# Packing eight units of a preparation into the rows of six, masks by ScalarE, and loads begun on ScalarE's queue

## The chip, the cores and the metric

The program runs on one core of one Trainium2 chip. Its engines work side by side, each through its own instructions in order: PE (TensorE, matmuls), DVE (VectorE, elementwise work and scans), ACT (ScalarE, copies out of PSUM, activations), POOL (GpSimd) and SP (SyncE, which issues DMAs). ACT can issue DMAs too; a DMA that ACT issues stands among its activations in the same order. The metric is the device time of one execution in microseconds (us), the median of several runs.

## The reference

A gated linear attention with a rank-one state correction (4 batches x 8 heads, 768 tokens, 40 channels) feeds a two-layer network with a spatial gate.

```python
for t in range(S):
    kt, vt, rt = (k[:, :, t], v[:, :, t], r[:, :, t])
    wt, at, bt = (w[:, :, t], a[:, :, t], b[:, :, t])
    y[:, :, t] = np.einsum('bhd,bhde->bhe', rt, state)
    Sa = np.einsum('bhde,bhe->bhd', state, at)
    state_decay = state * wt[:, :, None, :] - np.einsum('bhd,bhe->bhde', Sa, bt)
    state = state_decay + np.einsum('bhd,bhe->bhde', vt, kt)
...
h = np.maximum(x @ w_in, 0.0)
u, v = (h[..., :d_ff // 2], h[..., d_ff // 2:])
v_n = (v - mu) / np.sqrt(var + 1e-06)
v_s = np.einsum('ts,bsd->btd', w_spatial, v_n) + b_spatial[None, :, None]
return ((u * v_s) @ w_out).astype(np.float32)
```

Here x is y with its heads laid side by side, and mu and var are the mean and variance of v over its last axis.

## The kernel before

**Steps.** Phase 1 cuts the 768 tokens into chunks of 64 (C) and treats two batches at a time: 2 x 12 chunks are 24 steps (s, also q). A step has 16 heads, as 8 units (n) of two heads (par): one head lies in partitions 0 to 63, the other in 64 to 127. A head has 40 channels (E), so 40 of each 64 partitions carry data in everything that is laid out by channel; the loads of a preparation bring 48 rows per half, the last 8 being filling.

**Preparation of step q.** `prep_piece` loads the decays w and three other inputs (`oth`) of the step in six pieces of 16 rows. `scan1` and `scan2` form running products of w with two scans over 8 x 66 columns (`S`, `Et`; L292 and L301) and a reciprocal (L296); `at_mul` (L318) and `sl_mul` (L324) multiply `oth` by them into `at` and `sl`. All five run on DVE. `lprime` (L339) multiplies `sl` and `at` on PE into small triangles, and `lblock` (L349) copies them out of PSUM on DVE while it masks them with `maskl` and changes their sign. Four steps form a group; `invert` turns the group's 32x32 triangles into inverses on DVE, 30 rounds of two operations (L363, L367) between transposes. The input tiles `ein` are two, so the load of step q + 2 waits for `sl_mul` of step q. Results of eight steps are kept (`fifo`, and nine `Et`), so preparation runs up to eight steps ahead.

**The step itself.** Matmuls with the state, eviction by ACT, masking by POOL (`strict`, L406), and so on: `c_bp` (L545), `c_ff` (L563), `c_xx` (L581), `c_mp` and `c_y` (L641), with `c_y_out` (L654) writing y on DVE; the next step's `c_bp` follows. Blocks of the next step are made in between: `b_copy` (L392) copies `at` into `At` by DMA, `lin_load` (L381) and `vtok_load` (L384) bring the late inputs from HBM, `b_lka`, `b_h`, `b_tok` and others are matmuls with evictions by ACT.

**The network.** Its first layer (`m_v` L759, `m_u` L712) fills PE from step 11 on, four slots in a step and on beyond step 23; `vr` holds a normalised half before it is stored, in two buffers. `decode` turns the weights, which come as 64-bit numbers, into two floats each on DVE. Phase 2 does the spatial matmuls and the projection.

**Order.** It is written by hand: `at(t, fn, ...)` puts a function at a plan time, in units of a step; the plan is sorted and each engine gets its instructions in that order. `b_copy(q)` stands at q - 0.89, `lin_load(q)` at q - 1.80 and q - 1.66, `vtok_load(q)` at q - 0.52 and q - 0.38, all DMAs of a step on SP's queue. Preparations are placed by `PREP`: 4 and 5 in step 0, 6 and 7 in step 1, 8 and 9 in step 2, 10 and 11 in step 3, from 12 on one in a step. The network's loads and stores, `scn_load`, `scr_store` and `y_store` go through SP too.

Of the kernel before, what the change touches and what calls it, by code (L numbers as in the profile page):

```python
# [18 lines left out]
P = 128  # L19
# [9 lines left out]
EW = WF + 3 * NU * C  # L29
NR = C + E  # L30
# [187 lines left out]
def phase1(ctx, tc, early, late, vtok, win, xs, vns, uts, dscr):  # L218
# [12 lines left out]
    fifo = [pool(f"fifo{i}") for i in range(GS)]  # L231
# [4 lines left out]
    etp = pool("etp", 9)  # L236
# [15 lines left out]
    ein = [p.tile([P, EW], F32, name=f"ein{i}") for i, p in enumerate((pin, pin, extra, extra))]  # L252
# [16 lines left out]

    def prep_load(s, rows, cols=slice(0, EW), i=None, queues=(nc.sync, nc.sync)):  # L270
        t = ein[s % 2 if i is None else i]
        for par in range(2):
            o = par * 64
            queues[par].dma_start(out=t[o:o + rows, cols], in_=early[par, s, 0:rows, cols])

    def prep_piece(s, k):
        par, r = k % 2, k // 2 * 16
        o = par * 64 + r
        nc.sync.dma_start(out=ein[s % 2][o:o + 16], in_=early[par, s, r:r + 16])

    def scan1(s, i=None):
        t = ein[s % 2 if i is None else i]
        Et = etp.tile([P, WF], F32, name="Et")
        at = fifo[s % 8].tile([P, NU, C], F32, name="at")
        sl = fifo[s % 8].tile([P, NU, 2, C], F32, name="sl")
        wseg = t[:, 0:WF]
        oth = t[:, WF:].rearrange("p (q n c) -> p n q c", q=3, c=C)
        sx = pin.tile([P, WF], F32, name="S", bufs=2)
        sv = sx.rearrange("p (n c) -> p n c", c=WSEG)
        st["pre", s] = (Et, at, sl)  # L290
        st["raw", s] = (wseg, oth, sv)
        nc.vector.tensor_tensor_scan(  # L292
            out=sx[:, ::-1], data0=wseg[:, ::-1], data1=ends[:, ::-1],
            initial=0.0, op0=ALU.mult, op1=ALU.add,
        )
        nc.vector.reciprocal(out=eseg[:, :, 0:1], in_=sv[:, :, 1:2])  # L296

    def scan2(s):
        Et, at, sl = st["pre", s]
        wseg, oth, sv = st["raw", s]  # L300
        nc.vector.tensor_tensor_scan(  # L301
            out=Et, data0=wseg, data1=ends, initial=0.0, op0=ALU.mult, op1=ALU.add,
        )

    def scr_store(s):
        if s % CPB == 0:
            return
        sv = st["raw", s][2]
        sc = jit.tile([P, NU], F32, name="sc")
        nc.scalar.activation(sc, sv[:, :, 1], AF.Copy)  # L310
        for par in range(2):
            nc.sync.dma_start(out=scr[s, par], in_=sc[RR[par]])

    def at_mul(s, eng, ns=slice(0, NU)):
        Et, at, sl = st["pre", s]
        oth = st["raw", s][1]
        Ev = Et.rearrange("p (n c) -> p n c", c=WSEG)
        eng.tensor_tensor(out=at[:, ns], in0=oth[:, ns, 0], in1=Ev[:, ns, 0:C], op=ALU.mult)  # L318

    def sl_mul(s, eng, ns=slice(0, NU)):  # L320
        Et, at, sl = st["pre", s]
        wseg, oth, sv = st["raw", s]
        k = ns.stop - ns.start
        eng.tensor_tensor(  # L324
            out=sl[:, ns], in0=oth[:, ns, 1:],
            in1=sv[:, ns, 2:C + 2].unsqueeze(2).broadcast_to([P, k, 2, C]), op=ALU.mult,
        )

    def lprime(s, units=range(NU)):
# [4 lines left out]
        for n in units:  # L334
            for blk in range(2):
                for par in range(2):
# [3 lines left out]
                        pl[o:o + HB, n, :], lhsT=sl[PR[par], n, par, cs], rhs=at[PR[par], n, cs],  # L340
# [3 lines left out]
    def lblock(s):  # L344
        if s % GS == 0:
            st["Lc", s // GS] = inv.tile([P, GS * NU, HB], F32, name="Lc")
        Lc = st["Lc", s // GS]
        u0 = (s % GS) * NU
        nc.vector.tensor_tensor(  # L349
            out=Lc[:, u0:u0 + NU, :], in0=st.pop(("pl", s)),  # L350
            in1=maskl.unsqueeze(1).broadcast_to([P, NU, HB]), op=ALU.mult,
        )
# [27 lines left out]
    def lin_load(s, par):  # L380
        nc.sync.dma_start(out=lin[s % 2][RR[par], :, 0:LATE], in_=late[par, s])  # L381

    def vtok_load(s, par):
        nc.sync.dma_start(out=Rts[s % 2][par][PR[1 - par], :, C:], in_=vtok[s, par])  # L384

    def b_copy(s, par):
        if par == 0:
            At = [jat.tile([P, NU, C], F32, name=f"At{i}") for i in range(2)]
            tk = jit.tile([P, NU, 2, E], F32, name="tk")
            st["blk", s] = (At, Rts[s % 2], tk, xfs[s % 2])  # L390
        at = st["pre", s][1]
        nc.sync.dma_start(out=st["blk", s][0][par][PR[par]], in_=at[PR[par]])  # L392

    def b_lka(s):
        Et, at, sl = st["pre", s]
        pk = ps_k.tile([P, NU, C], F32, name="bk")
        for n in range(NU):
            for par in range(2):
                nc.tensor.matmul(  # L399
                    pk[PR[1 - par], n, :], lhsT=sl[PR[par], n, 1 - par, :], rhs=at[PR[par], n, :],  # L400
# [10 lines left out]
    def b_lka_out(s, par):  # L411
# [3 lines left out]
        if s in LKA_POOL:  # L415
            nc.scalar.activation(At[par][ev], pk[ev], AF.Copy)  # L416
            strict(At[par][ev], NU)
            return
        nc.vector.tensor_tensor(
            out=At[par][ev], in0=pk[ev],  # L420
            in1=maskp[ev].unsqueeze(1).broadcast_to([64, NU, C]), op=ALU.mult,
        )
# [12 lines left out]
    def b_h_out(s, par):  # L435
        ev = PR[1 - par]
        Rt = Rts[s % 2]
        if s in H_POOL:
            nc.scalar.activation(Rt[par][ev, :, 0:C], st["ph", s][ev], AF.Copy)
            strict(Rt[par][ev, :, 0:C], NU)  # L440
            return
        nc.vector.tensor_tensor(
            out=Rt[par][ev, :, 0:C], in0=st["ph", s][ev],
            in1=maskp[ev].unsqueeze(1).broadcast_to([64, NU, C]), op=ALU.mult,
        )
# [16 lines left out]
    def b_l21(s):  # L462
        Et, at, sl = st["pre", s]
        m1 = ps_k.tile([P, NU, HB], F32, name="bk")
        for n in range(NU):
            for par in range(2):
                o = (1 - par) * 64 + HB
                nc.tensor.matmul(
                    m1[o:o + HB, n, :], lhsT=at[PR[par], n, HB:], rhs=sl[PR[par], n, par, 0:HB],
# [116 lines left out]
    def c_xx_out(s, g):  # L586
# [3 lines left out]
        if s in TRI_POOL:  # L590
            for par in range(2):
                done = nc.scalar.activation(Rt[par][PR[par], gp], xx[PR[1 - par]], AF.Copy, scale=-1.0)  # L592
            marks["a", s] = done.ins
            for par in range(2):
                strict(Rt[par][PR[par], gp, 0:C], NP)
            return
        for par in range(2):
            nc.scalar.activation(Rt[par][PR[par], gp, C:], xx[PR[1 - par], :, C:], AF.Copy, scale=-1.0)
        for par in range(2):
            ur, ev = PR[par], PR[1 - par]  # L600
            nc.vector.tensor_tensor(
                out=Rt[par][ur, gp, 0:C], in0=xx[ev, :, 0:C],
                in1=maskn[ev].unsqueeze(1).broadcast_to([64, NP, C]), op=ALU.mult,
            )
# [41 lines left out]
    def c_y_out(s, g):  # L646
        gp, ns = grp(g)
        c = s % CPB
        Ev = st["pre", s][0].rearrange("p (n c) -> p n c", c=WSEG)
# [54 lines left out]
    def m_v(g, bq, i, k=0):  # L704
# [8 lines left out]
        vr = st["act"].tile([P, DH], F32, name="vr", bufs=2)  # L713
# [65 lines left out]
    H_POOL, LKA_POOL, TRI_POOL = range(0, 99), range(0, 99), range(0, 99)  # L779
# [47 lines left out]
    SCR, SLM = {4: 0.68}, {5: 0.83}  # L827
    PREP = {4: 0.03, 5: 0.45, 6: 1.03, 7: 1.45, 8: 2.03, 9: 2.45, 10: 3.03, 11: 3.45}
    for q in range(GS, NS):
        t = PREP.get(q, q - 8 + 0.01)  # L830
        at(t + 0.20, scan1, q)
        at(t + 0.28, scan2, q)
        at(SCR.get(q, t + 0.285), scr_store, q)
        at(t + 0.29, at_mul, q, AT_ENG)
        at(SLM.get(q, t + 0.30), sl_mul, q, SL_ENG)
        if q + 2 < NS:
            gap = 0.03 if q < 8 else 0.07 if q < 12 else 0.14
            for k in range(6):
# [10 lines left out]
    T_DEC, T_MOE = 4.2, 11  # L849
    for i in range(6):  # L850
        gen = decode(1 - i // 3, i % 3)
        for k in range(8):
            at(T_DEC + i + k * 0.10 - (0.9 if k == 0 else 0), step, gen)
    at(T_DEC + 5.9, open_act)
# [30 lines left out]
    with tc.manual_schedule():  # L885
# [4 lines left out]
        pads(v, ein[1])  # L890
# [7 lines left out]
        pads(p, ein[2])  # L898
        pads(p, ein[3])
        for q, cols in ((0, W), (1, W), (0, O), (1, O), (2, W), (2, O), (3, W), (3, O)):  # L900
            prep_load(q, 48 if q else 64, cols, q, qs)
# [4 lines left out]
        for m, val in ((maskp, 1.0), (maskn, -1.0)):  # L906
            p.memset(m, val)
            for rows in PR:
                p.affine_select(
                    out=m[rows], in_=m[rows], pattern=[[1, C]], base=0,  # L910
                    channel_multiplier=-1, compare_op=ALU.is_gt, fill=0.0,
                )
        for t in (Mc, *xfs):
# [23 lines left out]
        prep_load(4, 48)  # L937
# [14 lines left out]
        prep_load(5, 48)  # L952
# [73 lines left out]
```

## Time and profile before

| | us |
|---|---|
| median of 3 runs (663.11 to 670.05) | 667.58 |
| the profiled execution | 665.08 |
| its span, first to last instruction | 663.3 |
| busy in it: PE | 571.8 |
| DVE | 448.4 |
| ACT | 384.2 |
| POOL | 225.9 |

The clock granted to PE was 0.943 of full speed on average. An engine's busy time counts its instructions; the issuing of a DMA is counted as the queue's (SPq, ACTq), not as busy time. In rows of groups, the numbers after the bar are the group's busy time, the mean of one instruction in ns, and the idle time of the engine just before them with what ended it. In rows by time, the first number is the start from the span's begin, the second the duration. A row of a stage gives its window, its length, and for each engine the busy time and the instructions, then PE's clock, the DMA engines' busy share and GB/s. The busy shares are averages; what a stage is worth is read inside the stage.

### The profile page before, as it was taken

To read this page: it belongs to the slowest core of one execution; us is meant where nothing else is said; L and a number is where in the kernel's file an instruction comes from. 1 tells how busy PE (TensorE), PEld (TensorE's weight loads), DVE (VectorE), ACT (ScalarE), POOL (GpSimd) and SP (SyncE) were. 2 spreads that over 40 slices of the span, in tenths; PEclk is the share of its full clock that TensorE was granted. 3 is DMA by queue.
4 is the path that set the end of the run, shared out by engine and by line. 5 is a ranking of instruction groups with operands and counts; after the bars stand their busy time and mean duration, and the time that the engine had idled before them with its cause. 6 is when DMAs were issued, how large, how long until landed. Compare 5 with 4: busy or idle time off the path is not lost.

```text
span 663.3 us, 25848 instructions
## 1 busy us (share of the span) xinstructions
PE 571.8 (86%) x10960; PEld 518.3 (78%) x10960; DVE 448.4 (68%) x970; ACT 384.2 (58%) x860; POOL 225.9 (34%) x298
## 2 busy tenths in 40 slices
PE   1447885498777887999999999999989999999997
PEld 1437674487766776888888888888878999999997
DVE  8999789989999999488896677343384842332220
ACT  2135662377666775688878887888765543221212
POOL 6013330224332334144341332332354843352221
PEclk9967997789787898999999999999998999999999
DMA  8654778477555546657565365375395557150001
GB/s 199 121 107 67 134 152 147 70 175 155 135 127 115 131 117 120 142 127 172 154 190 148 86 173 144 90 198 132 89 262 182 162 155 240 61 157 31 31 31 59
DMA packets 106331, 87.68 MB, mean 132 GB/s; under 512 B 35496, under 2 KB 92072, under 8 KB 104296
## 3 DMA queue, kind: packets, MB, share of 16 engines
q1 hardware_dynamic: 105672, 84.31, 52.0%
q10 hardware_dynamic: 544, 1.72, 1.2%
q8 instruction: 86, 1.41, 1.0%
q14 instruction: 29, 0.24, 0.1%
HBM read 59.20 MB, written 20.50 MB: 120 GB/s over the span
## 4 chain that ended last, share of the span: by engine, by line
PE 63%; DVE 15%; DMA 7%; issue 6%; ACT 4%; SPq 3%; POOL 1%; DVEq 0%; ACTq 0%; POOLq 0%
PE po L199 6%; PE pv L759 6%; PE pv L712 6%; PE pg L179 5%; PE pg L180 5%; PE pg L181 5%; PE ch L563 4%; PE bp L545 4%; PE ch L581 4%; PE bk L429 2%; DMA ein<-in_early 2%; DVE itmp L363 2%; PE bk L451 2%; PE bk L399 2%; PE bp L641 2%
## 5 line engine op out<-in xcount | busy, mean ns | idle before, releaser
L406 POOL TENSOR_SCALAR_AFFINE_SELECT Rt<-Rt 64x512 f32<-64x512 f32 (+1 forms) x144 | 83.8, 584 | 156.2 <-ACT Rt L592 128.5
L406 POOL TENSOR_SCALAR_AFFINE_SELECT At<-At 64x512 f32<-64x512 f32 x48 | 41.5, 864 | 164.0 <-ACT At L416 151.9
L555 ACT ACTIVATE Rt<-bp 64x416 f32<-64x416 f32 x96 | 49.1, 511 | 56.2 <-PE bp L545 53.6
L363 DVE TENSOR_TENSOR itmp<-A 128x30 f32<-128x30 f32 (+9 forms) x180 | 66.5, 369 | 3.4
L179 PE MATMUL pg<-wsh,vh 128*128 128x384 f32 x192 | 65.4, 341 | 2.0 <-ACT vh L51 2.0
L545 PE MATMUL bp<-lin,Mc 40*64 40x104 f32 x768 | 47.3, 278 | 22.1 <-DVE y L654 19.8
L183 DVE TENSOR_TENSOR g<-pg,bb 128x384 f32<-128x384 f32 x32 | 17.8, 556 | 70.7 <-PE pg L181 68.4
L180 PE MATMUL pg<-wsl,vh 128*128 128x384 f32 x192 | 65.1, 339 | 0.0
L181 PE MATMUL pg<-wsh,vl 128*128 128x384 f32 x192 | 63.6, 339 | 0.0
L367 DVE TENSOR_TENSOR A<-A,itmp 128x30 f32<-128x30 f32 (+9 forms) x180 | 59.1, 328 | 6.2
L545 PEld LDWEIGHTS bp<-lin,Mc 40*64 40x64 f32 x768 | 40.7, 150 | 25.5 <-DVE y L654 22.7
L563 PE MATMUL ch<-Rt,At 128*64 128x104 f32 x768 | 48.0, 283 | 5.9 <-issue 4.8
L55 POOL TENSOR_TENSOR gl<-g,gh 128x384 fp32r<-128x384 f32 x32 | 33.0, 1035 | 58.1 <-ACT gh L51 58.1
L592 ACT ACTIVATE Rt<-ch 64x416 f32<-64x416 f32 x96 | 49.1, 511 | 4.6 <-PE ch L581 2.2
L563 PEld LDWEIGHTS ch<-Rt,At 128*64 128x64 f32 x768 | 42.2, 157 | 10.4 <-issue 7.1
L51 ACT ACTIVATE gh<-g 128x384 fp32r<-128x384 f32 x32 | 16.7, 521 | 54.3 <-DVE g L184 54.3
L339 PE MATMUL bk<-at,sl 64*32 64x32 f32 x1536 | 21.2, 203 | 26.5 <-DVE sl L324 20.7
L55 POOL TENSOR_TENSOR vl<-raw,vh 128x512 fp32r<-128x512 f32 x24 | 31.5, 1324 | 31.6 <-ACT vh L51 30.1
L581 PE MATMUL ch<-ffs,xf 64*64 64x104 f32 x768 | 41.7, 261 | 0.0
L339 PEld LDWEIGHTS bk<-at,sl 64*32 64x32 f32 x1536 | 17.7, 114 | 29.5 <-issue 14.4
L179 PEld LDWEIGHTS pg<-wsh,vh 128*128 128x128 f32 x192 | 36.6, 190 | 2.4 <-ACT vh L51 2.2
L630 DVE TENSOR_TENSOR Mc<-ch,scn 104x160 f32<-104x160 f32 x44 | 18.5, 436 | 29.0 <-PE ch L619 18.7
(132 smaller groups left out, 1497.8 us busy)
## 6 DMA issues: line engine op xcount, KB each, us to landing
ein<-in_early SPq DMA_DIRECT2D x108, 129.0 KB
lin<-in_late SPq DMA_DIRECT2D x48, 160.0 KB
At<-at SPq DMA_DIRECT2D x48, 128.0 KB
uts<-ur SPq DMA_DIRECT2D x48, 128.0 KB
vns<-vr SPq DMA_DIRECT2D x24, 256.0 KB
raw<-vns SPq DMA_DIRECT2D x24, 256.0 KB
ut<-uts SPq DMA_DIRECT2D x24, 256.0 KB
Rt<-in_vtok SPq DMA_DIRECT2D x48, 80.0 KB
```

What stands on the lines that cost most here:

```text
L55: eng.tensor_tensor(out=lo, in0=x, in1=hi.bitcast(F32), op=ALU.subtract)
L179: nc.tensor.matmul(pg, lhsT=vh[:, dc], rhs=w_h, start=(i == 0), stop=False)
L180: nc.tensor.matmul(pg, lhsT=vh[:, dc], rhs=w_l, start=False, stop=False)
L181: nc.tensor.matmul(pg, lhsT=vl[:, dc], rhs=w_h, start=False, stop=(i == NT - 1))
L363: nc.vector.tensor_tensor(out=tp, in0=A[:, k + 1:, k:k + 1].broadcast_to([P, m, k]), in1=A[:, k:k + 1, 0:k].broadcast_to([P, m, k]), op=AL ...
L367: nc.vector.tensor_tensor(out=A[:, k + 1:, 0:k], in0=A[:, k + 1:, 0:k], in1=tp, op=ALU.add)
L406: nc.gpsimd.affine_select(out=t, in_=t, pattern=[[0, k], [1, C]], base=0, channel_multiplier=-1, compare_op=ALU.is_gt, fill=0.0,)
L545: nc.tensor.matmul(bp[PR[par], q, :], lhsT=Mc[RR[par], n, :], rhs=li[RR[par], n, C:], start=(q == 0), stop=False, skip_group_check=True,)
L555: nc.scalar.activation(Rt[par][PR[par], gp, :], st["bp", g][PR[par]], AF.Copy)
L563: nc.tensor.matmul(ff[PR[1 - par], q, :], lhsT=At[par][:, n, :], rhs=Rt[par][:, n, :], start=True, stop=True,)
L581: nc.tensor.matmul(xx[ev, q, :], lhsT=xf[ev, n, :], rhs=ffs[ev, q, :], start=True, stop=True,)
L592: done = nc.scalar.activation(Rt[par][PR[par], gp], xx[PR[1 - par]], AF.Copy, scale=-1.0)
```

## The change

- **Packing.** From step 4 on, six units (NM) are laid out as before in rows 0 to 39 of each half; the other two units lie in the 24 rows that were empty, split into 24 and 16 rows in pieces of the unit's columns (24 rows of both units in one column block, 16 rows in the next). Scans and multiplications run over six units. Afterwards `relay` moves the two units to rows 0 to 39 with eight SBUF-to-SBUF DMAs per step on SP. Loads are ten pieces instead of six, of exactly 40 rows of data. `Et`, `at` and `sl` of a step are now one tile, with `at` and `sl` side by side for each unit; nine such tiles replace eight and nine. `scan2` has a small copy more (the full product into `Et`'s last column), and `scr_store` reads it there, later.
- **Triangles.** From step 4 on `lblock` is an ACT copy with scale -1. The upper part of the inversion's tile `A` is set to zero by five POOL memsets in its first round.
- **Queues.** For steps from 2 on, `lin_load`, `vtok_load` and `b_copy` are issued by ACT instead of SP, at the same plan times. `At` is a fixed pair of zeroed tiles, and 40 rows are copied.
- **Places.** The loads of steps 4 and 5 are issued near the start. Plan times of preparations 5 to 7, of `lprime` in them, of the inversions and of `decode` move by up to 0.25 of a step; pieces are issued closer together.
- **Others.** `vr` has three buffers. Branches that were never taken, with `maskp` and `maskn`, are gone.

```diff
+NM = 6
+WM = NM * WSEG
+PW = WM + 3 * NM * C
+TW = 3 * C
+NT9 = 9
...
+    def relay(s):
+        for t, m in halves(s):
+            for par in range(2):
+                o = par * 64
+                nc.sync.dma_start(out=t[o:o + 24, NM * m:], in_=t[o + E:o + C, 0:2 * m])
+                nc.sync.dma_start(out=t[o + 24:o + E, NM * m:], in_=t[o + E:o + E + 16, 2 * m:4 * m])
...
-            out=Et, data0=wseg, data1=ends, initial=0.0, op0=ALU.mult, op1=ALU.add,
-        )
+            out=halves(s)[1][0][:, 0:n * WSEG], data0=wseg, data1=ends[:, 0:n * WSEG],
+            initial=0.0, op0=ALU.mult, op1=ALU.add,
+        )
+        if s >= GS:
+            nc.vector.tensor_copy(out=Et[:, 0:n, C + 1], in_=sv[:, 0:n, 1])
...
+        else:
+            nc.scalar.activation(Lc[:, u0:u0 + NU, :], st.pop(("pl", s)), AF.Copy, scale=-1.0)
...
+        h = HB // 2 if g else 0
+        while h:
+            x = Af.rearrange("p (b x) -> p b x", x=2 * h * (HB + 1))[:, :, h:h + h * HB]
+            nc.gpsimd.memset(x.rearrange("p b (r c) -> p b r c", c=HB)[:, :, :, 0:h], 0.0)
+            h //= 2
...
-        nc.sync.dma_start(out=lin[s % 2][RR[par], :, 0:LATE], in_=late[par, s])
+        (nc.sync if s < 2 else nc.scalar).dma_start(
+            out=lin[s % 2][RR[par], :, 0:LATE], in_=late[par, s]
+        )
...
-        nc.sync.dma_start(out=st["blk", s][0][par][PR[par]], in_=at[PR[par]])
+        (nc.sync if s < 2 else nc.scalar).dma_start(out=Ats[s % 2][par][RR[par]], in_=at[RR[par]])
...
-        vr = st["act"].tile([P, DH], F32, name="vr", bufs=2)
+        vr = st["act"].tile([P, DH], F32, name="vr", bufs=3)
...
-    PREP = {4: 0.03, 5: 0.45, 6: 1.03, 7: 1.45, 8: 2.03, 9: 2.45, 10: 3.03, 11: 3.45}
+    PREP = {4: 0.03, 5: 0.49, 6: 0.95, 7: 1.4, 8: 2.03, 9: 2.45, 10: 3.03, 11: 3.45, 12: 4.01, 13: 5.01, 14: 6.01, 15: 7.01, 16: 8.01, 17: 9.01, 18: 10.01, 19: 11.01, 20: 12.01, 21: 13.01, 22: 14.01, 23: 15.01}
+    LPQ = {5: 0.89, 6: 0.9, 7: 0.8}
...
+    INV_T = {1: (2.3, 3.74), 2: (4.5, 7.6), 3: (8.0, 11.7), 4: (12.0, 15.74), 5: (16.0, 19.7)}
...
+        at(RLY.get(q, max(t + 0.36, OV.get((sl_mul, q), 0) + 0.005)), relay, q)
         if q + 2 < NS:
...
+            for k in range(10):
+                at(max(t + 0.40, OV.get((sl_mul, q), 0) + 0.01) + gap * k, prep_piece, q + 2, k)
...
+        for q in (4, 5):
+            for k in range(10):
+                prep_piece(q, k)
```

More of the change, by code (lines that the diff above doesn't have):

```diff
@@ L267, in phase1, with units, prep_load @@
     st, marks = {}, {}
-    def prep_load(s, rows, cols=slice(0, EW), i=None, queues=(nc.sync, nc.sync)):
-        t = ein[s % 2 if i is None else i]
+    def units(s):
+        return NU if s < GS else NM
+    def prep_load(s, rows, cols=slice(0, EW), queues=(nc.sync, nc.sync)):
         for par in range(2):
             o = par * 64
-            queues[par].dma_start(out=t[o:o + rows, cols], in_=early[par, s, 0:rows, cols])
+            queues[par].dma_start(out=nat[s][o:o + rows, cols], in_=early[par, s, 0:rows, cols])
@@ L276, in prep_piece @@
     def prep_piece(s, k):
[L277 to L287, printed above, removed]
+        par, k = k % 2, k // 2
@@ L294, in scan1 @@
             initial=0.0, op0=ALU.mult, op1=ALU.add,
         )
-        nc.vector.reciprocal(out=eseg[:, :, 0:1], in_=sv[:, :, 1:2])
+        nc.vector.reciprocal(out=eseg[:, 0:n, 0:1], in_=sv[:, 0:n, 1:2])
     def scan2(s):
@@ L414, in b_lka_out @@
         ev = PR[1 - par]
[L415 to L422, printed above, removed]
+        nc.scalar.activation(At[par][ev], pk[ev], AF.Copy)
+        strict(At[par][ev], NU)
     def b_h(s):
@@ L437, in b_h_out @@
         Rt = Rts[s % 2]
[L438 to L445, printed above, removed]
+        nc.scalar.activation(Rt[par][ev, :, 0:C], st["ph", s][ev], AF.Copy)
+        strict(Rt[par][ev, :, 0:C], NU)
     def b_tok(s, h):
@@ L589, in c_xx_out @@
         xx = st["xx", g]
[L590 to L596, printed above, removed]
         for par in range(2):
-            nc.scalar.activation(Rt[par][PR[par], gp, C:], xx[PR[1 - par], :, C:], AF.Copy, scale=-1.0)
+            done = nc.scalar.activation(Rt[par][PR[par], gp], xx[PR[1 - par]], AF.Copy, scale=-1.0)
+        marks["a", s] = done.ins
         for par in range(2):
[L600 to L604, printed above, removed]
+            strict(Rt[par][PR[par], gp, 0:C], NP)
     def c_mp(s, g):
@@ L852, in phase1 @@
         for k in range(8):
[L853 to L854 removed]
+            at(T_DEC[i] + k * 0.1 - (0.9 if k == 0 else 0), step, gen)
+    at(T_DEC[5] + 7 * 0.1 + 0.01, open_act)
     slots = [T_MOE + k // 4 + (M1, M2, M3, M4)[k % 4] for k in range(3 * NS)]
@@ L897, in phase1 @@
             )
-        pads(p, ein[2])
-        pads(p, ein[3])
+        pads(p, nat[2])
+        pads(p, nat[3])
+        for t in ein:
+            p.memset(t[:, 4 * WSEG:WM], 1.0)
+            p.memset(t[:, WM:], 0.0)
         for q, cols in ((0, W), (1, W), (0, O), (1, O), (2, W), (2, O), (3, W), (3, O)):
-            prep_load(q, 48 if q else 64, cols, q, qs)
+            prep_load(q, 48 if q else 64, cols, qs)
         for par in range(2):
@@ L904, in phase1 @@
             vtok_load(0, par)
+        for q in (4, 5):
+            for k in range(10):
+                prep_piece(q, k)
         make_identity(nc, ident)
[L906 to L913, printed above, removed]
+        for t in (Mc, *xfs, *Ats[0], *Ats[1]):
             p.memset(t, 0.0)
```

128 lines of the change are left out of this document (81 added, 47 removed).

## The prediction

> **What bounds the kernel now.** I read the page's 40 slices first, then a table of stages, then the waits and DVE's groups inside a stage, then DVE's order of time. The 24 steps of phase 1 have their borders at the writes of y (L654): steps 0 to 3 run from 54 to 134 us, steps 4 to 10 to 255, step 11 to 278, the rest to 490.
>
> ```profile
> PE   1447885498777887999999999999989999999997
> DVE  8999789989999999488896677343384842332220
> core 0: us, PE busy (x) PEld busy (x) DVE busy (x) ACT busy (x) POOL busy (x), PEclk, DMA share, GB/s
> 0.00:54.00 54.00, 19.34 (x517) 17.52 (x519) 47.84 (x98) 14.26 (x32) 14.56 (x32) 0.83 0.66 132
> 54.00:134.20 80.20, 56.25 (x1680) 49.04 (x1676) 70.39 (x128) 42.01 (x99) 24.51 (x30) 0.86 0.67 119
> 134.20:255.40 121.20, 101.26 (x2902) 89.61 (x2901) 114.81 (x230) 86.77 (x196) 39.89 (x57) 0.90 0.59 134
> 255.40:277.80 22.40, 17.86 (x345) 15.72 (x342) 13.91 (x26) 11.65 (x27) 6.60 (x10) 0.85 0.77 143
> 277.80:490.00 212.20, 209.81 (x4534) 181.68 (x4523) 137.18 (x356) 172.53 (x389) 73.17 (x111) 1.00 0.54 147
> ...
> 241.70:255.40 13.70, 12.85 (x406) 11.38 (x404) 13.15 (x30) 11.78 (x27) 5.76 (x9) 1.00 0.44 119
> ```
>
> DVE is busy 70.4 of 80.2 us in steps 0 to 3 and 114.8 of 121.2 in steps 4 to 10; PE is busy 209.8 of 212.2 from step 12 on. So DVE sets the pace up to 255 us and PE after it, and what DVE saves counts only before 255. The waits of the first two stages confirm it: PE waits for the last DVE operation of a step (the first row is of 54 to 134 us, the second of 134 to 255).
>
> ```profile
> PE bp L545 <- DVE y L654: 8.3, 2, 4.5
> ...
> PE bp L545 <- DVE y L654: 15.3, 10, 3.8
> ```
>
> **The change, part by part: DVE.** Between 54 and 255 us DVE prepares 15 steps (4 to 18). Their groups in that window, and one preparation in order of time:
>
> ```profile
> L301 DVE TENSOR_TENSOR_SCAN Et<-ein,ends 128x528 f32<-128x528 f32 x15 | 19.4, 1292 | 0.3
> L324 DVE TENSOR_TENSOR sl<-ein,S 128x1024 f32<-128x1024 f32 x15 | 19.1, 1276 | 0.0
> L292 DVE TENSOR_TENSOR_SCAN S<-ein,ends 128x528 f32<-128x528 f32 x15 | 18.8, 1252 | 1.6 <-DMA scr<-sc 1.0 <-DMA ein<-in_early 0.6
> L318 DVE TENSOR_TENSOR at<-ein,Et 128x512 f32<-128x512 f32 x15 | 12.7, 845 | 0.5
> L349 DVE TENSOR_TENSOR Lc<-bk,maskl 128x256 f32<-128x256 f32 x15 | 6.3, 418 | 4.0 <-PE bk L339 4.0
> ...
> 14.65 0.42 DVE L349 TENSOR_TENSOR Lc<-bk,maskl 128x256 f32<-128x256 f32 x1
> 14.99 1.25 DVE L292 TENSOR_TENSOR_SCAN S<-ein,ends 128x528 f32<-128x528 f32 x1
> ...
> 75.16 0.21 DVE L296 RECIPROCAL ends<-S 128x8 f32<-128x8 f32 x1
> ...
> 76.69 0.69 DVE L318 TENSOR_TENSOR at<-ein,Et 128x512 f32<-128x512 f32 x1
> 77.30 1.22 DVE L324 TENSOR_TENSOR sl<-ein,S 128x1024 f32<-128x1024 f32 x1
> ```
>
> The four large operations sum to 70.0 us and shrink to six of eight units. L318 to L324 shows the part that does not scale: 512 more columns cost 1.22 - 0.69 = 0.53, so 0.16 of the 0.69 is fixed. 60 operations x 0.16 = 9.6 fixed; a quarter of the other 60.4 is 15.1 saved (17.5 were nothing fixed). The copy of six elements into Et is new, 15 of them; nearest is the 0.21 of the reciprocal, and since ends overlap I take 0.15: 2.3 lost. L349 leaves DVE for ScalarE: the next instruction starts 0.34 after it, 15 x 0.34 = 5.1. Released on DVE: 15.1 - 2.3 + 5.1 = 17.9 us; by its 15 preparations and 15 masks, 9.2 in steps 0 to 3 (8 and 7 of them) and 8.7 in steps 4 to 10.
>
> In steps 4 to 10 there is cover for that: PE's 15.3 us of waiting on y is time in which everything but DVE was ready. I take 7.5 of 8.7 (bounds 0, and 8.7 plus 1.5 of the 4.0 us that DVE waits for PE before L349, which go with it).
>
> **SP's queue in steps 0 to 3.** Here the gain is less sure, since each preparation now issues 10 pieces and 8 relay copies where it issued 6 pieces, and SP goes through them in order. Issue times (ns: least, median, most):
>
> ```profile
> L279 SPq DMA_DIRECT2D ein<-in_early x108: 320/444/1912, 58.7 to 323.7; - x108
> L312 SPq DMA_DIRECT2D scr<-sc x44: 273/322/790, 22.0 to 339.2; - x44
> L381 SPq DMA_DIRECT2D lin<-in_late x48: 798/844/1309, 12.6 to 445.5; - x48
> L384 SPq DMA_DIRECT2D Rt<-in_vtok x48: 557/594/1542, 13.6 to 466.1; - x48
> L392 SPq DMA_DIRECT2D At<-at x48: 477/540/1864, 17.6 to 461.3; - x48
> ...
> 58.66 3.19 SPq L279 DMA_DIRECT2D ein<-in_early  x6
> ...
> 66.63 1.26 DVE L292 TENSOR_TENSOR_SCAN S<-ein,ends 128x528 f32<-128x528 f32 x1 [0.58 <-DMA ein<-in_early]
> ```
>
> New issues of 16 to 48 rows are nearest to L312's 40 rows; I take 0.35 (bounds 0.27 and 0.59): 18 x 0.35 = 6.3 against 6 x 0.444 = 2.7, 3.6 more per preparation. What moves away is 2 x (0.844 + 0.594 + 0.540) = 4.0 per step. From step 4, with one preparation each, SP is even; in steps 0 to 3, with two, it gains 3.2 per step. The pieces of step 6 can start only behind the eight copies of step 4: sl of step 4 ends about 57.5 instead of 58.6, copies until 60.3, pieces until 63.8. Before, issue ended at 61.85 and the scan started at 66.63, 4.8 later; now 68 at worst, 67 if smaller rows land a little sooner. So scans 6 and 7 start as late as before though DVE is done earlier; what is late next is the load. From the inversion of group 1 on, at most one preparation hangs on it. Of 9.2 I take 7 (bounds 0, and 9.2 plus the other 2.5 of L349's waits).
>
> The loads of steps 4 and 5 move ahead of the first At copy in SP's order (20 issues, about 7 us); covered by the inversion of group 0, which holds DVE until 54 us. Without that cover it would cost the 7. The new memsets on POOL lie there too.
>
> **The late tokens.** vtok is issued at plan time q - 0.52 behind everything else on SP; in step 11 that is on the path:
>
> ```profile
> 257.08 6.47 DMA Rt<-in_vtok
> ...
> 261.99 0.58 PE L563 MATMUL ch<-Rt,At 128*64 128x104 f32 x2 [3.42 <-issue]
> 263.68 3.00 PE L563 MATMUL ch<-Rt,At 128*64 128x104 f32 x30 [1.12 <-DMA Rt<-in_vtok]
> ```
>
> Plan time 10.48 lies near 248 us (step 10 is the last row of the first fence), and the transfer begins at 257: SP was late, and the landing took 6.47 more. On ScalarE's queue it goes out some 8 us earlier. PE waits 3.42 + 1.12 = 4.5; I take 4 (bounds 0, if it lands as late because the transfers themselves are dense, and 4.5).
>
> **ScalarE.** It gains 20 masks, 0.4 each by the row of L457 below, and those of steps 19 to 23 fall under PE. It also gains six issues per step, 4.0 us by the medians above; copies of At now read 64-element runs, nearer to lin's 0.844, which makes 4.6. What is queued behind them are the evictions that PE waits for. No row shows ScalarE issuing in a step; the start does:
>
> ```profile
> 0.81 0.55 ACTq L274 DMA_DIRECT2D ein<-in_early  x1
> 1.39 1.28 ACT L248 ACT_TABLE_LOAD   x1 [1.39 <-PEq L1013]
> 2.12 0.93 ACTq L274 DMA_DIRECT2D ein<-in_early  x2
> 2.68 0.20 ACT L248 ACTIVATE warm<-warm 128x1 f32<-128x1 f32 x1
> ...
> 5.00 0.32 ACTq L274 DMA_DIRECT2D ein<-in_early  x1
> ...
> 12.64 0.47 ACT L918 ACTIVATE lin<-ident 40x320 f32<-40x320 f32 x1 [9.76 <-DMA ein<-in_early]
> ...
> L457 ACT ACTIVATE tk<-bk 128x320 f32<-128x320 f32 x48 | 19.7, 435 | 8.0 <-PE bk L451 7.6
> ```
>
> Issues run at 0.81 and 2.12 while a table load and an activation that stand earlier in the source are still to be executed: the sequencer runs ahead by at least two instructions, about 1 us of evictions, longer than a 0.5 to 0.85 us issue. But L918 waits 9.76 us until issues that had to wait are out: an issue that blocks holds everything behind it. The six wait only for PE and copies of a step or more before, so I take 2 us in all (bounds 0 and 10: from 278 to 490 us, twelve steps, ScalarE's 172.5 + 12 x 4.0 + 5 x 0.4 = 222.5 would be 10.3 above the 212.2, were nothing overlapped).
>
> By the Trainium skill (Perfetto Trace Analysis, "DMA Instruction — HWDGE (DVE, Sync)") an issue keeps the issuing sequencer until its descriptors are made, with the generator locked for one issuer at a time. The trace agrees so far as two issues took 0.93 while SP issued too, and one took 0.32 later. By that rule alone, with nothing running ahead, all 21 x 4.0 = 84 us would be paid and the sum would be 734. The same page ("DVE / Act Engine Instruction") has the sequencer push an activation into a wait queue and go on, which is what the rows of the table load show; by that the sum stays 652.
>
> **Smaller parts.** Inversions get five POOL memsets each (0.1 to 0.2 us each by the 128x64 row) between the transpose and the next DVE operation, one plan step of about 1 us away: 0.5 lost in all, bounds 0 and 5. The third vr buffer acts where PE is full: 0. maskp and maskn were used by no instruction of a step: 0. Matmuls over 40 rows instead of 64 stream the same columns: 0.
>
> ```profile
> L907 POOL MEMSET maskn<- 128x64 f32 x1 | 0.2, 151 | 0.1
> ```
>
> **Sum.** 7 + 7.5 + 4 - 2 - 0.5 = 16 gained. The profiled execution took 665.1 (span 663.3), so 649; the median of the three runs is 667.6, 2.5 above it, so 651.6, and I forecast 652.
>
> **Rivals.** *Loads bound steps 0 to 3.* Copies and pieces hold SP; if an issue costs 0.59 instead of 0.35, a preparation's 18 take 10.6 and the two of a step 21 us, as long as the step itself. Then nothing is gained there: 652 + 7 = 659. For it: scan 6 already waits for its load. Against it: SP is free again after step 3. *DVE is relieved and the time stays.* The chain of PE and ScalarE is as long as the step once issues and masks lie in it; then only part of the vtok wait goes, 665. Against it: step 10, 241 to 255 us, took 13.7 with the same chain, the others about 17.5. *ScalarE is blocked: slower.* Where the sequencer's lead is used up, an issue delays the eviction behind it. If a share of the issue time is exposed in the 21 steps 2 to 22, its price is that share of 21 x 4.0 = 84 us. The gains of 18 are gone at 22%, one per cent slower is reached at 30%, and with 40% exposed it ends at 667.6 - 18 + 34 = 683. For it: L918's wait, and evictions that follow an issue directly. Against it: the two instructions of lead.
>
> **How the numbers follow.** Forecast 0.60 (641 to 659 by the bounds: all upper ones together 641), loads 0.12, time stays 0.14, ScalarE blocked 0.14. One per cent, 6.7 us, is about what a measurement of this kernel can tell from no change. Faster by more: 0.60 and most of the loads case, 0.70; slower: most of the blocked case, 0.13; within: 0.17. Range 641 to 668: it leaves out the blocked case and little else.
>
> **What would show it.** DVE's groups L292 to L324 25% fewer columns and about 3.5 us per preparation; PE's wait on y smaller but still there up to step 10; step 11 without the wait for vtok; the stage from step 12 as long as before (212 us less a little). Wrong if DVE's idle time before scans 6 to 9 grows by more than 7 us, or if PE waits for ScalarE in steps 12 to 22.

## The result and the profile after

| | us | ratio to before (95% interval) |
|---|---|---|
| before, median of 4 runs beside it | 666.82 | |
| after, median of 4 runs (736.31 to 746.84) | 742.63 | 1.115 (1.109 to 1.121) |
| after, the profiled execution (span 734.6) | 736.31 | |

The kernel became 11% slower, where 2% faster was forecast. Here and below, medians are of all runs and ratios of the fast ones alone, that is without runs more than 1.5% above their kernel's fastest; only for e6 (721.3 without its two slow runs) and e11 (722.5 without one) does this move the median of a run by more than 1 us. First the 40 slices of after:

```profile
PE   1469566856696979787999889999998999999997
DVE  8995219962879795766657646663354353233221
PEclk9976567685859796998889999999998999999999
```

Between the start and the end of phase 1, the gaps of PE lie mainly in slices 5 to 19, and the granted clock is low in most slices from 3 to 21. The table of stages, by the writes of y as before (steps 0 to 3, 4 to 10, 11, 12 to 23):

```profile
core 0: us, PE busy (x) PEld busy (x) DVE busy (x) ACT busy (x) POOL busy (x), PEclk, DMA share, GB/s
54.00:154.65 100.65, 71.84 (x1662) 62.95 (x1663) 60.86 (x129) 44.21 (x103) 19.21 (x35) 0.66 0.39 95
154.65:308.48 153.83, 117.60 (x2882) 102.52 (x2877) 105.63 (x229) 91.83 (x205) 37.32 (x67) 0.78 0.44 112
308.48:327.02 18.54, 16.14 (x368) 14.29 (x361) 13.15 (x25) 11.69 (x27) 6.25 (x10) 1.00 0.49 125
327.02:564.52 237.50, 223.59 (x4538) 191.12 (x4529) 134.64 (x364) 176.36 (x401) 73.58 (x122) 0.95 0.48 134
```

Against the same stages of before, 20.5, 32.6 and 25.3 us were lost and 3.9 won in step 11. DVE is busy 9.5 and 9.2 us less in the first two stages, as intended, but no engine fills them any more. Over the four stages PE is busy 44 us longer for the same matmuls, 429.2 us at a mean clock of 0.84 against 385.2 at 0.94. Busy time times clock is about the same (361 and 362), so the lower clock accounts for the 44 us. DVE's groups of the 15 preparations (54 to 308 us) show the part that went right:

```profile
L365 DVE TENSOR_TENSOR pre<-ein,S 128x768 f32<-128x768 f32 x15 | 15.8, 1054 | 0.0
L338 DVE TENSOR_TENSOR_SCAN pre<-ein,ends 128x396 f32<-128x396 f32 x15 | 14.7, 982 | 0.2
L328 DVE TENSOR_TENSOR_SCAN S<-ein,ends 128x396 f32<-128x396 f32 x15 | 14.7, 980 | 9.0 <-DMA ein<-in_early 9.0
L358 DVE TENSOR_TENSOR pre<-ein,pre 128x384 f32<-128x384 f32 x15 | 9.0, 600 | 4.0 <-DMA pre<-pre 3.5
L343 DVE COPY pre<-S 128x6 f32<-128x6 f32 x15 | 3.2, 212 | 0.5
```

The waits from 67 to 354 us (steps 1 to 12) show who waits now:

```profile
PE bk L492 <- ACT At L468: 23.3, 8, 7.3
...
ACT At L468 <- DMA At<-pre: 16.2, 3, 7.2
...
ACT xf L807 <- DMA pre<-pre: 12.8, 3, 5.0
...
ACT xf L564 <- DMA At<-pre: 9.9, 1, 9.9
...
PE bp L586 <- DVE y L685: 7.8, 2, 6.9
```

PE's wait on y fell from 8.3 and 15.3 us (54 to 255 us of before) to 7.8. In its place PE waits for ScalarE, and ScalarE, whose work here is mostly evictions out of PSUM, "waits for DMAs", some of which its evictions don't read at all. Its order of time shows what that is (ACTq is its sequencer issuing):

```profile
76.02 2.63 ACTq L445 DMA_DIRECT2D At<-pre  x2
78.69 1.21 ACT L468 ACTIVATE At<-bk 64x512 f32<-64x512 f32 x2 [7.86 <-DMA ein<-in_early]
...
106.92 1.71 ACTq L445 DMA_DIRECT2D At<-pre  x2
108.68 0.59 ACT L468 ACTIVATE At<-bk 64x512 f32<-64x512 f32 x1 [7.21 <-DMA At<-pre]
```

The eviction at 78.69 stands behind two At issues that could not go out before a piece of `ein` had landed, a load for another step. The compiled kernel tells why, and the trace records the same semaphores with each instruction: every transfer of SyncE and ScalarE signals its landing on one of eight semaphores (called slots here), dealt out in turn to both queues together in the order of the program, and an issue first waits until the last transfer of its slot has landed.

```
SyncE    L290 ein1 <- in_early   slots 4, 5
SyncE    L292 ein1 <- in_early   slots 6, 7
SyncE    L352 scr  <- sc         slots 0, 1
SyncE    L295 ein1 <- in_early   slots 2, 3
ScalarE  L445 At00 <- pre2       slot 4: waits for the first L290 above
SyncE    L301 ein1 <- in_early   slot 5
ScalarE  L445 At10 <- pre2       slot 6: waits for the first L292 above
```

So ScalarE's issue waits for whatever SyncE began some eight transfers earlier in the program. The first At issue of this list began at 76.02 us, and the last landing on its slot is recorded at 75.99. An issue could also be held by what its own transfer needs, such as a buffer that PE still reads. The trace speaks against that: after 60 us, 21 of ScalarE's issues in after began more than 0.3 us after everything else of ScalarE had ended, 52 us in all, and before each of them the last event that it waited for was a landing on its own slot, never an engine. SyncE's queue, in turn, became long:

```profile
L313 SPq DMA_DIRECT2D pre<-pre x80: 729/766/1160, 57.5 to 410.0; - x80
L314 SPq DMA_DIRECT2D pre<-pre x80: 519/531/1447, 58.3 to 410.8; - x80
L301 SPq DMA_DIRECT2D ein<-in_early x80: 298/371/1254, 22.0 to 371.8; - x80
```

An issue of a relay copy takes 0.77 us (24 rows) or 0.53 us (16 rows), where 0.35 was taken.

### The profile page after: what moved, and what is told of

It is laid out like the page before. It is cut to its first block, busy times and chain, and to the rows that moved or that the text cites. A ratio compares the mean times of both kernels' runs of the same rounds, so it can differ in the third digit from the quotient of the medians.

```text
span 734.6 us, 26081 instructions
## 1 busy us (share of the span) xinstructions
PE 615.7 (84%) x10960; PEld 552.9 (75%) x10960; DVE 416.8 (57%) x970; ACT 394.0 (54%) x880; POOL 220.6 (30%) x335
## 5 line engine op out<-in xcount | busy, mean ns | idle before, releaser
L459 POOL TENSOR_SCALAR_AFFINE_SELECT Rt<-Rt 64x512 f32<-64x512 f32 (+1 forms) x144 | 76.0, 528 | 178.2 <-ACT Rt L632 140.8
L459 POOL TENSOR_SCALAR_AFFINE_SELECT At<-At 64x512 f32<-64x512 f32 x48 | 38.0, 793 | 197.0 <-ACT At L468 195.4
L492 PE MATMUL bk<-ident,pre 128*128 128x128 f32 x192 | 33.3, 314 | 35.3 <-ACT At L468 24.0
L596 ACT ACTIVATE Rt<-bp 64x416 f32<-64x416 f32 x96 | 49.0, 511 | 23.5 <-PE bp L586 21.2
L492 PEld LDWEIGHTS bk<-ident,pre 128*128 128x128 f32 x192 | 23.5, 157 | 41.9 <-ACT At L468 26.4
L622 PE MATMUL ch<-ffs,xf 64*64 64x104 f32 x768 | 50.8, 295 | 2.0 <-ACT ffs L612 2.0
L380 PE MATMUL bk<-pre 40*32 40x32 f32 x1536 | 25.5, 218 | 29.9 <-DVE pre L365 19.9
L622 PEld LDWEIGHTS ch<-ffs,xf 64*64 64x64 f32 x768 | 44.8, 163 | 3.4 <-ACT ffs L612 2.2
L380 PEld LDWEIGHTS bk<-pre 40*32 40x32 f32 x1536 | 22.3, 128 | 33.2 <-DVE pre L365 12.3
L468 ACT ACTIVATE At<-bk 64x512 f32<-64x512 f32 x48 | 28.3, 589 | 32.9 <-DMA At<-pre 16.2
L604 PE MATMUL ch<-Rt,At 128*64 128x104 f32 x768 | 44.5, 272 | 0.0
```

The costliest lines, as they stand in the source:

```text
L380: nc.tensor.matmul(pl[o:o + HB, n, :], lhsT=sl[RR[par], n, par, cs], rhs=at[RR[par], n, cs], start=True, stop=True,)
L459: nc.gpsimd.affine_select(out=t, in_=t, pattern=[[0, k], [1, C]], base=0, channel_multiplier=-1, compare_op=ALU.is_gt, fill=0.0,)
L492: nc.tensor.transpose(pt[:, n, :], sl[:, h * NP + n].rearrange("p q c -> p (q c)"), ident)
L596: nc.scalar.activation(Rt[par][PR[par], gp, :], st["bp", g][PR[par]], AF.Copy)
L622: nc.tensor.matmul(xx[ev, q, :], lhsT=xf[ev, n, :], rhs=ffs[ev, q, :], start=True, stop=True,)
```

## Experiments

The first theory, A, later called K: ScalarE's issues wait through the shared slots for SyncE's transfers and hold its evictions. Its rivals: B, the issuing itself (4.4 us per step) is what ScalarE lacks; C, relays and pieces make the operands late, whichever queue starts the other transfers. After the first four runs C was split into S, SyncE's queue is overlong and all that stands in it comes late, and P, it is the landing of the copies, whoever begins them. The "all on SyncE" kernels below put `nc.sync` back in `lin_load`, `vtok_load` and `b_copy`. Lengths by stage, from the writes of y in each profiled run (us):

| run | median, ratio | steps 1-4 | 5-11 | 12-16 | 17-23 |
|---|---|---|---|---|---|
| before | 665 to 667 | 86.4 | 126.0 | 92.5 | 119.6 |
| after | 742.6, 1.115 | 121.0 | 139.2 | 111.8 | 125.7 |
| e1: six on SyncE | 745.7, 1.126 (1.121 to 1.131) | 117.3 | 153.0 | 117.2 | 122.6 |
| e2: before, six on ScalarE | 698.0, 1.053 (1.048 to 1.059) | 96.7 | 135.5 | 100.3 | 121.6 |
| e5: six on GpSimd | 697.1, 1.052 (1.048 to 1.057) | 103.4 | 121.4 | 110.9 | 122.0 |
| e6: relays on GpSimd | 727.7, 1.088 (1.080 to 1.096) | 96.6 | 158.1 | 99.0 | 127.6 |
| e7: relays on GpSimd, six on SyncE | 674.6, 1.017 (1.010 to 1.024) | 88.8 | 115.4 | 100.9 | 126.6 |
| e8: no relays | 717.3, 1.078 (1.072 to 1.084) | 99.3 | 151.7 | 96.8 | 130.8 |
| e9: no relays, six on SyncE | 657.8, 0.988 (0.985 to 0.991) | 84.4 | 116.2 | 93.7 | 122.3 |
| e10: as e8, pieces on GpSimd | 679.2, 1.020 (1.010 to 1.029) | 90.2 | 127.2 | 97.4 | 124.0 |

One profiled execution stands behind each row of lengths. The kernel before and e17 are the same up to step 16, and their step 11 took 22.4 and 17.2 us; e15 and e16 are the same up to step 10, and their steps 1 to 4 took 88.0 and 91.6. So differences of some 5 us between stages say little by themselves.

**e1 and e2: each half of the change alone.**

```diff
-        (nc.sync if s < 2 else nc.scalar).dma_start(out=Ats[s % 2][par][RR[par]], in_=at[RR[par]])
+        nc.sync.dma_start(out=Ats[s % 2][par][RR[par]], in_=at[RR[par]])
```

> The changed kernel with its loads of lin and vtok and the copies At begun on SyncE's queue again, packing, relays and masks left as they are. Theory A (the transfers of both queues share a few completion slots; an issue on ScalarE waits until an older transfer of SyncE, late behind the relays, has landed, and the evictions behind it wait with it): ScalarE is freed, so its idle time before At L468 and xf L807 and L564 that ends at a transfer (about 40 us between 67 and 230 us) goes; SyncE carries some 4 us more per step, which costs part of it in steps 1 to 5; 675 us (655 to 700). Theory B (the issuing itself, 4 to 5 us per step, holds ScalarE): 655 to 675 as well. Theory C (relays and ten pieces make the operands late, whichever queue starts the other transfers): no gain, 735 to 760, since SyncE has more to do.

> The kernel before, with nothing changed but that the loads of lin and vtok and the copies At of steps 2 and later are begun on ScalarE's queue. A: SyncE has six pieces and no relays, so the older transfers have mostly landed when ScalarE wants their slot; some waits in steps 1 to 4, and the wait of step 11 for vtok goes (4 us): 667 us (655 to 690). B: 21 steps x 3 us or more, 710 to 740. C: 663 (the vtok wait goes and nothing else).

e1 was a miss for A: with ScalarE free of issues the kernel is as slow, 745.7, as C had it. SyncE's order of time in it shows one preparation's load and another's relays:

```profile
64.10 0.70 SPq L290 DMA_DIRECT2D ein<-in_early  x2
64.85 0.90 SPq L292 DMA_DIRECT2D ein<-in_early  x2
65.79 1.70 SPq L295 DMA_DIRECT2D ein<-in_early  x2
67.53 1.63 SPq L301 DMA_DIRECT2D ein<-in_early  x4
69.28 0.79 SPq L313 DMA_DIRECT2D pre<-pre  x1
...
74.35 0.54 SPq L314 DMA_DIRECT2D pre<-pre  x1
```

From 64.10 to 74.89 are 10.8 us for 18 issues; two preparations and the six others make more than a step. Who waits for it, in steps 1 to 4 of e1:

```profile
DVE S L328 <- DMA ein<-in_early: 34.5, 6, 9.9
...
PE bk L380 <- DMA pre<-pre: 22.7, 9, 6.1
```

e2 lost 33 us, more than A's 690 and short of B's 710: the queues hurt each other even with six pieces and no relays. Both halves cost, and they don't add: the move takes some 4 us of issuing per step off SyncE, which e1 lacks.

**e5, e6, e7: the transfers on a third queue.** In e5 GpSimd begins the six, in e6 the relays, in e7 the relays with the six on SyncE.

```diff
-                nc.sync.dma_start(out=t[o:o + 24, NM * m:], in_=t[o + E:o + C, 0:2 * m])
+                nc.gpsimd.dma_start(out=t[o:o + 24, NM * m:], in_=t[o + E:o + C, 0:2 * m])
```

> The changed kernel with the six transfers of each step (lin, vtok, At) begun by GpSimd in place of ScalarE, at the same places of the order. In the compiled kernel these have completion slots of their own, not those of SyncE. A: ScalarE no longer waits for slots; GpSimd's issue time is not known from any run, so 685 (655 to 720). B: about the same, 655 to 720. C: 735 to 760. A and B differ in that by A the transfers of lin and vtok begin at once, by B only ScalarE's time is less.

> The changed kernel with the eight relay copies of a preparation begun by GpSimd in place of SyncE; the six transfers of a step stay with ScalarE. The relays then have other completion slots, and SyncE is rid of 8 x 0.65 = 5.2 us per preparation and of the wait for DVE's sl. A: the transfers eight places back have landed in time, so ScalarE's idle time before At L468 goes from some 22 us (67 to 230 us) to under 6: 680 us (650 to 705). B: ScalarE issues as before, 730 to 750. C: relays still have to land before the matmuls; if their landing is what costs, 720 to 750.

> The changed kernel with the relay copies begun by GpSimd and lin, vtok and At begun by SyncE: ScalarE begins no transfer of a step. Theory S (SyncE's queue is the bound of steps 1 to 4: 18 issues of a preparation take some 9.5 us of it, and two preparations and the six others more than a step): SyncE keeps ten pieces and the six, 4.3 + 4 us where all 24 took 13.5, so the loss of 79 us of the kernel with all on SyncE shrinks to 20 or less: 675 us (660 to 690). Theory P (what costs is the landing: a copy that must go out after sl and land before the matmuls, whoever begins it): 715 to 745. If ScalarE's issues cost something of their own beside SyncE's length (theory K), this kernel is the fastest with packing so far, below the 697 of the six on GpSimd.

e7 came to 674.6, S's number: 71 us of e1's loss go when eight issues per preparation leave SyncE, though the copies still go out after `sl` and land before the matmuls. P falls as the main cost; the 17 us between e7 and e9 below, where the copies are left out, may be the landing or GpSimd's issuing. e5 lies in its range; e6 missed (680 expected): with the relays gone from SyncE, ScalarE's six still cost 47 us (721.3 against e7's 674.6; two expectations below take 728 and so 53).

**e8, e9, e10: without relays.** These leave out the relay copies, so units six and seven are computed from old data of their buffers.

```diff
-        at(RLY.get(q, max(t + 0.36, OV.get((sl_mul, q), 0) + 0.005)), relay, q)
```

> The changed kernel with all transfers begun by SyncE and without the relay copies: units six and seven of the operands of steps 4 to 23 are left as they lie in their buffers, so this computes those units from old data. S: SyncE has ten pieces where the kernel before had six, DVE is 18 us shorter: 660 us (645 to 680). P says the same here (no landing to wait for): 645 to 680. Were ten small pieces enough to hold SyncE, or DVE's scans late for another reason (theory L, loads themselves): 700 or more.

> The changed kernel as it is (lin, vtok and At begun by ScalarE) but without the relay copies, as in the run beside it. S alone: 650 to 670, at or below the one with all on SyncE. K (an issue on ScalarE waits for the landing of an older transfer of SyncE, and holds the evictions behind it, even where SyncE isn't overlong): the 33 us that moving the queue cost the kernel before come on top: 680 to 705.

> As the run without relay copies and with the six transfers begun by ScalarE (717 us), but the ten pieces of a preparation are begun by GpSimd too (from step 6 on), so they too have other completion slots than ScalarE's six; units six and seven again keep old data. K by the slots (an issue on ScalarE waits for the landing of a piece of SyncE some eight transfers back): without pieces among those the waits go, 685 us (665 to 700), in spite of some 5 us more of GpSimd per preparation. If it is the issuing itself that costs ScalarE (4.4 us per step, as long as its room in a step): 710 to 735.

e9, the packing without its relays, is 1.2% faster than before. e8 differs from it in nothing but who begins the six: 717.3 against 657.8, 59.5 us, more than K's upper end of 705. e10 differs from e8 only in that GpSimd, whose transfers have eight slots of their own, begins the pieces in place of SyncE, and 38 of the 59.5 us go; ScalarE issues as many transfers as in e8, and SyncE's relief isn't the reason, since e9 is fast with the pieces and the six all on SyncE. That is K and not B. Counted as in after, ScalarE's idle time before issues that waited for a slot is 26 us in e8 and 5 in e10 (22 in e2, 35 in e6). B also fails within after itself: in steps 17 to 21, without preparations, ScalarE issues its six per step all the same, and they took 87.2 us against 86.7 before. In these 87 us ScalarE is busy for 72 and issues for 23, so the issuing runs beside its activations in part.

**e11, e12: which of the six.** With e7 as base (674.6), lin and vtok or At alone begun by ScalarE.

> Relays on GpSimd, At begun by SyncE, lin and vtok by ScalarE. All six on SyncE gave 675, all six on ScalarE 728. K: in the run with all six on ScalarE the idle time of its sequencer just before an issue was 13.7 us for lin, 14.6 for vtok and 1.7 for At, so nearly all of the 53 us stays: 710 (695 to 728). By issue time alone (lin 33 us and vtok 26 of 97): 32 of the 53, 707. The two differ in the other run.

> Relays on GpSimd, lin and vtok begun by SyncE, At by ScalarE. K: the At issues wait little: 680 (672 to 690). By issue time alone (At 38 us of 97): 21 of the 53, 695 (688 to 705).

723.8 (ratio 1.085, 1.074 to 1.095) and 681.8 (1.025, 1.017 to 1.033): nearly all of the loss is with the loads of lin and vtok, not in proportion to issue time. ScalarE's idle time before issues that waited for a slot goes the same way, 38 and 4 us.

**e13: GpSimd in the kernel before, and a mixture.**

> The kernel before, with lin, vtok and At of steps 2 and later begun by GpSimd, whose transfers have completion slots of their own in the compiled kernel. Beside it stands the kernel before with the same six begun by ScalarE, 698 us. K by the slots: GpSimd's issues wait for none of SyncE's transfers, so nothing but their own time on GpSimd is paid: 665 us (655 to 680). If it is not the slots but that such an issue takes 0.6 to 0.85 us of an engine that works in the step's chain: 685 to 705 here too, since the triangles that PE waits for are GpSimd's.

> A kernel put together from what the runs showed: preparations 4 to 11 (two to a step) and 19 to 23 stay unpacked, with pieces of 16 whole rows as before; only 12 to 18, one to a step where DVE is the bound, are packed, and their relay copies begun by GpSimd; all six transfers begun by SyncE; masks by ScalarE; two vr buffers and one of sc, for room. Steps 5 to 11 of the kernel with relays on GpSimd and the six on SyncE took 115 us against 126 before; steps 12 to 16 should be as before (93 us) and steps 1 to 4 near the 86 of before: 656 (648 to 667), faster than before. If the gain of steps 5 to 11 came from the packed preparations 4 to 11 too: 665.

The first came to 680.3 (1.024, 1.018 to 1.029), between the two cases: a good half of e2's loss goes when GpSimd, with slots of its own, begins the six; the rest stays. The mixture missed: 673.1 (1.012, 1.006 to 1.019). Steps 5 to 11 took 122.2, not 115, and steps 1 to 4 took 94.0; why the latter were longer than before wasn't tried; some 4 us may be the spread told below the table.

**e14, e15, e16: the terms of gain alone, on the kernel before.**

```diff
-        nc.sync.dma_start(out=Rts[s % 2][par][PR[1 - par], :, C:], in_=vtok[s, par])
+        (nc.scalar if s == 11 else nc.sync).dma_start(out=Rts[s % 2][par][PR[1 - par], :, C:], in_=vtok[s, par])
```

> The kernel before, with one thing changed: the two loads of vtok of step 11 are begun by ScalarE. It tries the term of 4 us by itself. The term: the wait of 4.5 us of PE in step 11 goes and nothing else moves, 663 us against 667 (ratio 0.994). K: the two issues may wait for an older transfer of SyncE and hold ScalarE once, up to 4 us, and then the gain is gone: 665 to 669.

> The kernel before, with the masks L349 of steps 4 and later left to a copy of ScalarE and five memsets of GpSimd per inversion, nothing else. By the terms, DVE is rid of 15 x 0.34 = 5.1 us before step 11 and ScalarE gains 20 x 0.4: 663 us (659 to 667). If the inversions now wait for the memsets or for ScalarE's copy: 667 to 673.

> The kernel before with the masks as in the run beside it, and the two loads of vtok of step 11 begun by GpSimd. If both terms hold and add: 659 us (655 to 663), faster than the kernel before by about 1%. If one of them fails: 663.

e14 is the clearest of all: two issues moved, and the kernel is 1.0% slower (672.1, ratio 1.0104, 1.0069 to 1.0139), more than K's range of 665 to 669. ScalarE, then SyncE, then PE, in order of time:

```profile
250.13 0.77 ACT L457 ACTIVATE tk<-bk 128x320 f32<-128x320 f32 x2
258.38 0.59 ACTq L384 DMA_DIRECT2D Rt<-in_vtok  x1
259.01 1.15 ACT L776 ACTIVATE xf<-XT 128x256 f32<-128x256 f32 x3 [8.12 <-DMA scr<-sc]
...
255.53 0.83 SPq L312 DMA_DIRECT2D scr<-sc  x2
...
260.61 1.45 PE L487 MATMUL bk<-XT,l 32*32 32x32 f32 x32 [7.72 <-ACT l L477]
```

What the issue waits for last is its slot. SyncE, busy with the network's loads, begins the transfer that holds it only at 255.53; its last landing is recorded at 258.36, the issue begins at 258.38, and ScalarE, which had been done at 250.9, goes on: 8.12 us for its evictions, 7.72 for PE. Step 10 grew from 13.7 to 24.2 us. Step 11 took 16.5 where 22.4 stand for before, but e17 has 17.2 for it with vtok on SyncE. e15, the masks alone, is 663.6 (0.997, 0.994 to 1.000), about its expectation, and not told apart from no change with certainty. e16 adds vtok of step 11 on GpSimd and beats both kernels with nothing left out: 661.7 (0.993, 0.990 to 0.996). It lies 1.9 us below e15, so vtok's term of 4 came in by about half.

**e17: what a pause of PE costs.**

```diff
+    def stall(s):
+        for _ in range(8):
+            nc.scalar.activation(st["ffs", 0], st["ffs", 0], AF.Copy)
+    for s in range(17, 23):
+        at(s + 0.342, stall, s)
```

> The kernel before, with eight idle copies of ScalarE (ffs onto itself, 0.51 us each, 4.1 in all) in each of steps 17 to 22, where PE is busy 104.2 of 104.8 us at a granted clock of 1.00 and ScalarE has some 3 us of room. It is to show whether waits of PE cost more than their length. If they cost their length alone: PE's busy time stays 104 us and the clock 1.00, each step grows by at most 4.1 us, 667 to 685 us. If PE's pauses lower the granted clock (as the stages with many pauses had 0.6 to 0.9): PE busy 110 or more over these steps at a clock below 0.97, and more than the pauses is lost.

Steps 17 to 22, first of the kernel before, then of e17:

```profile
370.34:475.12 104.78, 104.23 (x2196) 90.32 (x2195) 53.45 (x153) 86.65 (x196) 34.04 (x56) 1.00 0.50 138
...
371.70:511.17 139.47, 115.39 (x2195) 100.16 (x2195) 52.77 (x153) 111.73 (x244) 34.16 (x56) 0.90 0.37 103
```

The six steps grew by 34.7 us, 10 more than all the copies take (48 x 0.51 = 24.6), and PE was busy 11.2 us longer at a clock of 0.90. PE's idle time grew by 23.5, the length of the copies at most; the 11.2 come on top, and 104.2 / 0.90 = 115.8 is PE's busy time there. The whole kernel took 701.5 (1.054, 1.048 to 1.060). The Trainium skill (TensorE: Matmul & The Clock Gate, "What's actually happening") has PE's clock fall to half after an idle window of about 3.4 us and come back after as long a busy one. The trace agrees so far as the clock falls with pauses of a few us, 1.00 to 0.90.

## Why the prediction was wrong

**The step that failed first** is that of ScalarE: "The six wait only for PE and copies of a step or more before, so I take 2 us in all". They also wait, by shared slots, for SyncE's transfers. Measured by moving only the six: 33 us (e2 on the kernel before), 47 (e6 on e7), 59.5 (e8 on e9). The row that spoke of it was in the prediction: L918 waits 9.76 us "until issues that had to wait are out: an issue that blocks holds everything behind it". The question left out was what else an issue may wait for. The rival with ScalarE blocked had the right sign and place, but priced it as a share of issue time, with 84 us as the whole; the price is the time until an older transfer of SyncE has landed, 52 us of idle ScalarE in after.

By the Trainium skill's rule that was weighed (Perfetto Trace Analysis, "DMA Instruction — HWDGE (DVE, Sync)"), issue time kept from ScalarE gave 734, near the 742.6. The agreement is by chance: steps 17 to 21 pay 0.4 us for 30 such issues, which take 23 us.

**The second** is SyncE: "I take 0.35 (bounds 0.27 and 0.59): 18 x 0.35 = 6.3". The relays take 0.77 and 0.53, pieces 0.35 to 0.85 each in the rows of e1, and 18 took 10.8 us in e1. That is the upper bound's 10.6, and the rival on loads had it; but its price of 7 us counted only the gain that scans would miss. The same queue holds the relays that the matmuls need, in e1 also At, lin and vtok, and with all of them it cost 81 us net of what packing saved (e1). In after, the copies of step 4 were out at 63.1 us where 60.3 was worked out, the pieces of step 6 at 67.7 where 63.8, and scan 6 began at 69.4 where 68 was the worst case (its own terms, 63.8 + 4.8, give 68.6). "From step 4, with one preparation each, SP is even" fell with it.

**The third** is not in the prediction at all: PE's clock. Of 74.5 us lost up to the end of step 23, 30.5 are more idle time of PE and 44 are matmuls that ran at a lower clock. e17 shows that pauses of PE bring the clock down. The sum had every wait at its length.

**What held.** The four DVE operations fell from 70.0 to 54.2 us, 15.8 saved for 15.1; the copy took 0.21 each, 3.2 instead of 2.3. But these were terms of a bound that no longer stood. Step 11 fell from 22.4 to 18.5, 3.9 for the 4 taken for vtok; that is luck, since it took 17.2 in e17 with nothing changed up to there. Where the bound does stand (e9, with vtok on SyncE and no relays), packing, masks and plan gained 4.1 us in steps 0 to 3 (7 forecast for DVE) and 7.6 in steps 4 to 11 (7.5 forecast for DVE), and 3.8 were lost from step 12 on, the cause of which wasn't tried. So the DVE terms came to 11.7 of 14.5 us up to step 11. Steps 4 to 11, first of before, then of e9:

```profile
134.19:277.81 143.62, 119.15 (x3241) 105.35 (x3240) 128.74 (x255) 98.43 (x222) 46.49 (x66) 0.89 0.62 136
...
130.12:266.13 136.01, 122.53 (x3254) 108.05 (x3254) 119.07 (x253) 101.77 (x230) 44.86 (x76) 0.88 0.50 129
```

DVE is busy 9.7 us less and the stage is 7.6 shorter. In steps 0 to 3 DVE is busy 9.4 less and the stage 4.1 shorter: there more than half of what DVE saved became idle time of DVE.

Both signs that the prediction named came, in after. DVE's idle time before the scans at L328 is 9.0 us, in two waits of 2.5 and 6.4 before scans 6 and 7. And from step 12 to 22 PE waits for ScalarE, some 10 us in all:

```profile
PE bk L528 <- ACT l L518: 4.6, 4, 3.1
```

**Open.** Which of the waits in after bring the clock down can't be told apart there; e17 only shows that a pause costs more than its length. The waits for slots account for a part of each loss as idle time of ScalarE (22 of 33 us in e2, 26 of 59.5 in e8); that the rest is the clock and the later operands is argued, not shown. What is left of e8's loss in e10 (21 us) may be GpSimd's added work; slots shared with the transfers that SyncE still begins make 5 us of it. In the runs without relays, a quarter of the units hold old or zero data; whether that alone changes the granted clock wasn't tried.

## What to carry to other kernels

Before moving DMA issues to another engine, look up in the compiled kernel which completion semaphore each one waits for: an engine that issues waits, and its later work with it, for the last transfer on that semaphore, whichever engine began it. Count a queue by its measured issue times, shape by shape, against the length of a step, and price an overfull queue by everything that stands in it. Price a new wait of PE above its length, because the clock falls with it.

## What the runs showed of the hardware

- SBUF-to-SBUF copies of 24 rows took 0.77 us to issue on SyncE and those of 16 rows 0.53, at either width (132 or 384 columns); loads of 24 rows from HBM took 0.37 for three runs per row. On GpSimd both copies took 0.51.
- The Trainium skill (DMA: Bandwidth & Descriptors, "Issuing engines are not separate DMA queues") says that beginning transfers on several engines saves only the sequencer's time. Here it saved nothing and cost 33 to 59.5 us, since the compiled kernel shares its slots between two of them; on GpSimd, with slots of their own, the six cost 15 (680.3 against 665.1).
- Pauses of PE of 3.6 to 4.8 us in each of six steps lowered the granted clock to between 0.86 and 0.93 in each of them and made the same 2195 matmuls 11% longer.
